# Three PSUM banks shared by all askers, queries by eight heads through DRAM, and a new instruction order in a two-attention kernel

## The chip, the cores and the metric

The kernel runs on one core of one Trainium2 chip. The metric is the device time of one launch in microseconds. The shown time of the kernel before is the median of three runs, 826.01 us (825.94 to 826.19). One execution was profiled; its own time and span are in the table below.

## The reference

Two attentions over the same input `x` (2048 tokens, width 512, 32 heads of 16) are mixed token by token:

```python
g = sigmoid((x * gate_w).sum(-1, keepdims=True))
a = softmax(q k^T / 4) v, per head, over all 2048 keys, then @ A_wo
b = softmax over 8 neighbours (token, token-2, ... token-14) of q k / 4, weighted v, then @ B_wo
out = g * a + (1 - g) * b
```

`q`, `k`, `v` come from `x @ A_wqkv` and `x @ B_wqkv`. `B_x` is not used. All inputs are bf16.

## The kernel before, in words

**Attention A** is cut into 32 periods: 4 blocks of 512 queries, and in each 8 groups of 4 heads. A period needs 64 units; a unit is one head with 128 keys and 512 queries. For a unit TensorE multiplies `kt_all` with `qt` into PSUM (scores, 32 rows per head), an engine takes the exponential, and TensorE multiplies the result with `vp_all` into the accumulator of the period. ScalarE takes most units: sets of three and two in turn stand in two PSUM rings (`rA`, three banks, and `rB`, two), and one ACTIVATE turns a set into a `pT` buffer (three buffers for each ring, so set k writes the buffer of set k-6). VectorE takes 339 units in all (3 to 12 in a period, `n_dve`): it scales the scores of one unit and adds a constant so that, read as bf16 bits, they are a rough exponential (`p1`, out of PSUM bank `D` into `dt_a` or, late, `wkv`), and for three units together it makes three shifted copies (`sh`, into `pd_a`); the four copies are multiplied with four weighted versions of V (`vd_all`), which smooths the error of the rough exponential. At a period's end VectorE transposes the accumulator (`accT`), takes reciprocals (`rden`), GpSimd scales (`ott`), and VectorE transposes back (`oat`).

**Queries.** `q_proj` (L721) makes a period's `qt`: 16 matmuls of 32 columns, in which every head's 16 columns stand twice (`wq2`); VectorE copies the result out of PSUM and masks the sign of the second copy with `qmask` (it carries an upper bound of the scores).

**Attention B** goes in 16 tiles of 128 tokens (`b_tile`). TensorE projects keys, values and queries; VectorE copies them out; keys and values go to a DRAM scratch `kv_scr` and come back shifted by 0 to 14 tokens (`ksh`, `vsh`, four shifts in one load, three buffers `gat`). GpSimd forms the products with the query, adds them up in halves to logits `lg`, subtracts the maximum; ScalarE takes the exponential; GpSimd multiplies with the gate and the reciprocal, forms the products with V and adds them up to `obb`. TensorE transposes `obb`, and the output projection adds it to attention A's part.

**Order.** Every instruction belongs to an `Op` with an engine, a duration, a due time, dependencies and buffers. `list_schedule` (L159) runs once while the kernel is built: it goes forward in planned time, and of the operations of an engine that can start it takes the one due first. It puts in matmuls with zeros where TensorE would idle. The result is a fixed order on each engine; chained helpers (L323, and L332 for matmuls) force it, so nearly all instructions carry these two lines. An engine whose next instruction must wait holds up all behind it. The DMAs of the kernel are all issued by SP, in its own fixed order.

**PSUM.** Eight banks: five for the rings, one `acc` (the accumulator), one `D` (scores for VectorE) and one `misc` (all projections, transposes, outputs, zeros).

Of the kernel before, what the change touches and what calls it, by code (L numbers as in the profile page):

```python
# [20 lines left out]
    dve_tiles=3,  # L21
# [15 lines left out]
DEXP = 56  # L37
NV = 4
NGR = 3
NPD = 3  # L40
# [4 lines left out]
NDE = 2  # L45
NDL = 4
SPREAD = (0.75, 0.8)
STEP = 32.0
WEIGHTS = (0.240234375, 0.2021484375, 0.169921875, 0.142578125)
# [10 lines left out]

class Tok:
    def __init__(self, res):
        self.res, self.ops = res, []


class Op:

    def __init__(self, eng, occ, fn, dl, deps=(), alloc=(), use=(), lat=None, rel=0.0, name="",
                 mode="f", js=(), full=0.0, fill=False, scores=None, after=(), ride=False, parts=None):
        self.scores, self.ride, self.parts = scores, ride, parts  # L70
# [17 lines left out]
GFIRST = -300.0  # L88
PRE = 0.14
GP = lambda kind, n: [(False, PRE), (True, NS[kind] * n)]  # L90
# [11 lines left out]
P1D, SHD, LASTD, PO1D = -100.0, 2.0, 200.0, 300.0  # L102
# [56 lines left out]
def list_schedule(ops, zeros):  # L159
# [15 lines left out]

    def avail(o):
        t = o.ready
        for tk in o.alloc:
            r = tk.res
            n = len(r.order)  # L180
            if n >= r.cap:
                for u in r.order[n - r.cap].ops:
                    if u.done is None:
                        return INF
                    t = max(t, u.end + SELF[u.eng] if u.eng == o.eng else u.done)
        return t

    arr = Array()

    def start(e, o):  # L190
# [5 lines left out]
        t0, end, _, _ = arr.plan(o, t)  # L196
        rides = o.mode == "r" and arr.mode == "r" and end < arr.end + 0.05
        return t0, o.dl + ((ALONE if o.ride else KEEP) if o.mode != arr.mode else 0.0) - (RIDE if rides else 0.0)
# [3 lines left out]
    while len(out) < len(ops):  # L202
# [24 lines left out]
        if e == "pe":  # L227
            tz, n = arr.idle(o, t)
            if n > 0:
                z = zeros(n)  # L230
                tz = max([tz, avail(z)] + [u.t for tk in z.alloc[0].res.order[-2:] for u in tk.ops if u.done is not None and u.t < t])
                if tz + n * PASS + (0.0 if o.mode == "c" else SWITCH) <= t + 0.05:
                    for tk in z.alloc:
                        tk.res.order.append(tk)
# [3 lines left out]
        for tk in o.alloc:  # L238
            tk.res.order.append(tk)
# [16 lines left out]
        out.append(o)  # L256
        for s_ in succ.get(o, ()):
            left[s_] -= 1
            if left[s_] == 0:
                s_.ready = max([s_.rel] + [d.end + SELF[d.eng] if d.eng == s_.eng else d.done for d in s_.deps] + [d.t for d in s_.after])  # L260
# [5 lines left out]
def kernel(  # L266
# [29 lines left out]

    def misc_ps(shape, dtype=FP32, tag="misc"):
        return ps.tile(shape, dtype, tag=tag, bufs=1, name="misc_ps")
# [50 lines left out]
    def op(eng, occ, fn, dl, **kw):  # L349
        if any(tk.res is res.get("misc") for tk in kw.get("use", ())):  # L350
# [7 lines left out]
    def tok(tag, cap):  # L358
        if tag not in res:
            res[tag] = Res(cap)  # L360
        return Tok(res[tag])
# [30 lines left out]
    for pi, (own, groups) in enumerate(seq):  # L392
        n = sum(len(g) for g in groups)
        left = [(gi, u_) for gi, g in enumerate(groups) for u_ in g]
        total, taken = len(own), 0
        for t, j in own:
# [4 lines left out]
            if left and n - len(left) < n * taken / (SPREAD[n // 10] * total) and all(u_[0] == pi for u_ in cur):  # L401
                js = [u_[2] for u_ in cur]
                pick = [x for x in left if x[0] == left[0][0] and x[1][1] not in js]
                if not pick and n - len(left) + 1 < n * taken / (SPREAD[n // 10] * total):
# [12 lines left out]
    wq2 = const.tile([128, DC, H, 2, DH], BF16, name="wq2")  # L417
# [6 lines left out]
    NH = NG // 2  # L424
    woarr = const.tile([128, NH, D], BF16, name="woarr")
    ident = const.tile([128, 128], BF16, name="ident")
    identf = const.tile([128, 128], FP32, name="identf")
    rowc = const.tile([128, 3], FP32, name="rowc")
    wts = const.tile([128, NV], BF16, name="wts")
# [7 lines left out]
    vd_all = const.tile([128, NV, NTD, H, DH + 1], BF16, name="vd_all")  # L437
# [5 lines left out]
    pd_a = const.tile([128, NPD * NGR * ROW], BF16, name="pd_a")  # L443
# [3 lines left out]
    pd_bufs = [pd_a[:, k_ * NGR * ROW:(k_ + 1) * NGR * ROW].rearrange("p (q n) -> p q n", q=NGR) for k_ in range(NPD)]  # L447
    stage = [pd_a[:, k_ * DC * D:(k_ + 1) * DC * D].rearrange("p (c n) -> p c n", c=DC) for k_ in range(2)]
    ott2 = const.tile([128, 2, BPC, 32], BF16, name="ott2")
# [3 lines left out]
    e1 = const.tile([128, NT], FP32, name="e1")  # L453
    d1 = const.tile([128, NT], FP32, name="d1")

    def init_dve():
# [9 lines left out]
        for m in range(NV):  # L466
            V.memset(wts[:, m:m + 1], WEIGHTS[m] * 2.0 ** -DEXP)

# [10 lines left out]
    def init_pool2():  # L479
        make_identity(nc, identf[:])  # L480
# [19 lines left out]
    def load_x(sc):  # L500
        def s():
            xl = work.tile([128, W // 2, D], BF16, name="xld", tag="gat", bufs=NGA) if sc < NGA else stage[1]
# [4 lines left out]
    wst = {}  # L507

    def load_w(part):
        def s():  # L510
            if part == 0:
                wst["q"] = stage[0]
                out = wst["q"]
            else:
                out = wkv[:, :, (part - 1) * D:part * D]
# [18 lines left out]
    tw = tok("pd", NPD)  # L534
# [7 lines left out]
    o_wq = op("sp", 0.5, load_w(0), -8.5, lat=12.5, alloc=[tw])  # L542
# [13 lines left out]
    def q2(E, i):  # L556
        def s():
            a0 = wst["q"][:, :, 4 * i * DH:4 * (i + 1) * DH]
# [6 lines left out]
    o_q2 = [op("dve", 0.5, q2(V, 0), 0.0, deps=[o_wq], use=[tw])]  # L565
    o_q2 += [op("pool", 1.5, q2(G, i), 4.0 + i, deps=[o_wq, o_k3[1]], use=[tw]) for i in range(1, NG)]
# [5 lines left out]
    o_warm = op("pe", 4.0, warm, -9.0, deps=[o_init_d], alloc=[tok("misc", 1)])  # L572
# [34 lines left out]
    def k_proj(i, sc, tag, dl, rel=0.0):  # L607
        st = {}
        tk = tok(tag, 1)
# [16 lines left out]
    def k_bound(i, dl):  # L626
        st = {}
        tk = tok("acc" if i == 0 else "misc", 1)
# [28 lines left out]
    for i in range(NG):  # L657
        o_kc[i] = []
        for sc in range(NC):
            if i == 0:  # L660
                o_kc[i].append(k_proj(i, sc, ("misc", "acc", "D", "misc")[sc], -2.0 + sc))
# [7 lines left out]
    def v_proj(h0, h1, tb, TB, tag, dl, rel=0.0):  # L669
        n = (h1 - h0) * DH  # L670
        st = {}
        tk = tok(tag, 1)
# [18 lines left out]
        def evd():  # L691
# [3 lines left out]
                            in0=_ap(vp_all[:, t0, h0, 0:1], [list(vp_all[:].ap[0]), [0, NV], [H * (DH + 1), nt], [1, n_]]),  # L695
                            in1=_ap(w, [list(w.ap[0]), [1, NV], [0, nt], [0, n_]]), op=ALU.mult)
# [7 lines left out]
        if nt > 0:  # L704
            d = op("dve", 0.0, evd, dl + 2.0, deps=[c], parts=TT(NV * nt * (h1 - h0) * (DH + 1)))
# [15 lines left out]
    def q_proj(pi, tag, dl, rel=0.0):  # L721
        c_, i = periods[pi]
        st = {}
        tk = tok(tag, 1)
        tq = tok("qt", 3)
        q_tok[pi] = tq

        def part(c0, c1):
            def s():
                if c0 == 0:  # L730
                    st["p1"] = misc_ps([128, QW], tag=tag)
                    qt_tiles[pi] = work.tile([128, QW], BF16, name="qt", tag="qt", bufs=3)
# [17 lines left out]
    for pi in range(1, NP):  # L750
        q_proj(pi, "misc", S0[pi] - 10.0, rel=S0[pi - 1] - 6.0 if pi > 1 else Q1REL)
# [3 lines left out]
    tzp, tzr = tok("misc", 1), tok("misc", 1)  # L755
# [10 lines left out]
    def zsig():  # L766
        A.activation(out=e1[:], in_=st_g["zp"][:, 0:NT], func=ACT.Exp, scale=-1.0)

    def zgate():
        V.tensor_scalar_add(out=d1[:], in0=e1[:], scalar1=1.0)  # L770
        V.reciprocal(out=g_sp[:], in_=d1[:])
        V.tensor_tensor(out=omg[:], in0=e1[:], in1=g_sp[:], op=ALU.mult)

    def zrows():
        st_g["zr"] = misc_ps([128, NT, TPC])
        for s_ in range(TPC):
            for j in range(4):
                mm(st_g["zr"][32 * j:32 * j + 32, :, s_], identf[:, 32 * s_:32 * s_ + 32], g_sp[:], True, True,
# [16 lines left out]
    WH = W // 2  # L795
# [3 lines left out]
    def b_tile(t):  # L799
# [26 lines left out]
        tk = tok("misc", 1)  # L826
# [3 lines left out]
        tk = tok("misc", 1)  # L830
        a = op("pe", WAVE(2), proj("pv", 2, 0), tb - 32 - KB, full=2, deps=[o_bw] + o_xt[cb], alloc=[tk], rel=rel)
# [8 lines left out]
        tk = tok("misc", 1)  # L840
# [12 lines left out]
        tlg, tob, tbb = tok("lg", 2), tok("ob", 1), tok("obb", 1)  # L853
# [4 lines left out]
        def logits_mul(hf, wp, w_, c0):  # L858
            def s():
                if hf == 0 and wp == 0 and w_ == 0 and c0 == 0:  # L860
                    st["lg"] = work.tile([128, H, W], FP32, name="lg", tag="lg", bufs=2)
                if w_ == 0 and c0 == 0:
                    st["prod", hf, wp] = work.tile([128, WP, D], FP32, name="prod", tag="prod", bufs=2)
# [29 lines left out]
        def sm_sub():  # L893
            lg, mx = st["lg"], st["mx"]
            mx_bc = _ap(mx[:], [list(mx[:].ap[0]), [1, H], [0, W]])
            G.tensor_tensor(out=lg[:], in0=lg[:], in1=mx_bc, op=ALU.subtract)
# [12 lines left out]
        def sm_gate():  # L909
            rr = st["rr"]  # L910
            G.tensor_scalar(out=rr[:], in0=rr[:], scalar1=omg[:, t:t + 1], scalar2=None, op0=ALU.mult)

        def sm_mul():
            ex, rr = st["lg"], st["rr"]
            rr_bc = _ap(rr[:], [list(rr[:].ap[0]), [1, H], [0, W]])
            G.tensor_tensor(out=ex[:], in0=ex[:], in1=rr_bc, op=ALU.mult)
# [3 lines left out]
        def av_mul(hf, wp, w_, c0):  # L920
            def s():
                if wp == 0 and w_ == 0 and c0 == 0:
                    key = ("ob", "obb")[hf]
                    st[key] = work.tile([128, D], (FP32, BF16)[hf], name=key, tag=key, bufs=1)
                if w_ == 0 and c0 == 0:
                    st["prod", hf, wp] = work.tile([128, WP, D], FP32, name="prod", tag="prod", bufs=2)
# [4 lines left out]
                G.tensor_tensor(out=st["prod", hf, wp][:, w_, c0:c0 + HB].rearrange("p (h d) -> p h d", d=DH),  # L931
                                in0=st["vsh", hf][:, wp + w_, c0:c0 + HB].rearrange("p (h d) -> p h d", d=DH),
                                in1=attn_bc, op=ALU.mult)
            return s, "bf", HB

        def av_add(hf, wp, c0, k_):
            def s():
                prod, ob = st["prod", hf, wp], st["ob"]
                cs = slice(c0, c0 + HB)
                if not hf and not wp:  # L940
                    G.tensor_tensor(out=ob[:, cs], in0=prod[:, 0, cs], in1=prod[:, 1, cs], op=ALU.add)
                elif k_ == 0:
                    G.tensor_tensor(out=prod[:, 0, cs], in0=prod[:, 0, cs], in1=prod[:, 1, cs], op=ALU.add)
                else:
# [425 lines left out]
```

## Time and profile before

| what | value |
|---|---|
| median of three runs | 826.01 us |
| the profiled execution | 826.04 us |
| its span, first to last instruction | 824.3 us |
| granted TensorE clock, mean | 0.994 |
| exponentials of attention A on ScalarE | 684, in 778.8 us busy |
| first of them starts, last of them ends | 19.67 us, 815.5 us |
| products and adds of 128x256 on GpSimd (`prod<-prod`, `prod<-ksh,qb`, `prod<-vsh,lg`) | 352, 256 and 256 times |
| shifts of VectorE (`pd_a`) | 195 and 144 times, 941 and 945 ns |
| transfers | 47.37 MB, 57 GB/s on average |

Busy times are the union of an engine's records. TensorE's matmuls are pipelined, so a busy TensorE need not be at its peak. "Idle before, <- releaser" is the time in which an engine did nothing ahead of an instruction, put down to whatever came last of what it waited for. Idle time matters only on the chain that ends last.

### The profile page before, as it was taken

The numbers are of one execution on the slowest core, as the hardware profiler recorded it, in microseconds if no ns is written. First come the engines' busy times: TensorE is split into PE (matmuls) and PEld (weight loads), VectorE is DVE, ScalarE is ACT, GpSimd is POOL, SyncE is SP. The second block draws the span as 40 slices with busy tenths as digits, with TensorE's granted clock in tenths as the row PEclk, the third lists the DMA queues.
The fourth block names the chain that finished last, engine by engine and source line by source line (L and its number), as shares of the span: only waits on it lengthen the run. The fifth ranks groups of instructions, "written<-read, shape, count | busy, mean of one in ns | idle before, by whom it ended". The sixth has DMA issues, their size and how long they took to land.

```text
span 824.3 us, 18657 instructions
## 1 busy us (share of the span) xinstructions
PE 777.9 (94%) x7314; PEld 247.4 (30%) x7358; DVE 706.3 (86%) x1111; ACT 785.9 (95%) x706; POOL 720.4 (87%) x1196
## 2 busy tenths in 40 slices
PE   7999999999999999999999999999999999999996
PEld 4333433333322222222222222222222222222231
DVE  5456876788978999989999899999989899998987
ACT  3899999999899899999999999999999999999995
POOL 5097999999999999899999999899999999899960
PEclk9899999999999999999999999999999999999999
DMA  9203020112111220211112111211111211110000
GB/s 296 78 3 116 2 90 28 65 52 65 57 48 65 65 66 28 63 53 47 63 35 77 57 50 51 65 53 49 43 52 54 82 34 65 52 52 27 27 1 26
DMA packets 44440, 47.37 MB, mean 57 GB/s; under 512 B 2352, under 2 KB 41776, under 8 KB 44352
## 3 DMA queue, kind: packets, MB, share of 16 engines
q1 hardware_dynamic: 44352, 46.18, 17.6%
q8 instruction: 57, 0.93, 0.5%
q14 instruction: 31, 0.25, 0.1%
HBM read 39.85 MB, written 6.32 MB: 56 GB/s over the span
## 4 chain that ended last, share of the span: by engine, by line
ACT 47%; PE 31%; issue 18%; DVE 2%; DMA 1%; SPq 0%; DVEq 0%; ACTq 0%
ACT pT L323 46%; PE acc L332 11%; PE ring L332 9%; PE misc_ps L332 8%; PE D L332 3%; DMA xld<-in_A_x_dram 1%; ACT lg L323 1%; DVE pd_a L323 0%; DVE kt_all L323 0%; PE pxt L584 0%; PE misc_ps L1011 0%; DVE dt_a L323 0%; DVE qt L323 0%; DVE vp_all L323 0%; DVE wkv L323 0%
## 5 line engine op out<-in xcount | busy, mean ns | idle before, releaser
L323 ACT ACTIVATE pT<-ring 128x1536 bf16<-128x1536 f32 (+1 forms) x684 | 778.8, 1319 | 20.5 <-PE acc L332 14.0
L332 PE MATMUL ring<-qt,kt_all 32*128 32x512 bf16 x1709 | 272.0, 382 | 28.4 <-ACT pT L323 19.2
L323 POOL TENSOR_TENSOR prod<-prod 128x256 f32<-128x256 f32 x352 | 235.6, 677 | 13.2
L332 PE MATMUL acc<-pT,vp_all 128*17 128x512 bf16 (+1 forms) x1709 | 189.0, 385 | 0.3 <-DVE accT L323 0.2
L323 POOL TENSOR_TENSOR prod<-ksh,qb 128x256 f32<-128x256 bf16 x256 | 166.5, 673 | 22.5 <-DMA ksh<-kv_scr 21.7
L323 DVE TENSOR_SCALAR pd_a<-dt_a 128x1536 uint16<-128x1536 uint16 x195 | 180.4, 941 | 1.2
L332 PEld LDWEIGHTS <-kt_all 32*128 32x128 bf16 x2048 | 91.2, 91 | 294.1 <-issue 285.2
L323 DVE TENSOR_SCALAR dt_a<-D 128x512 uint16<-128x512 f32 x195 | 132.7, 680 | 39.2 <-PE D L332 38.5
L323 POOL TENSOR_TENSOR prod<-vsh,lg 128x256 f32<-128x256 bf16 x256 | 162.0, 652 | 0.0
L323 DVE TENSOR_SCALAR pd_a<-wkv 128x1536 uint16<-128x1536 uint16 x144 | 131.0, 945 | 1.9 <-PE acc L332 0.3
L332 PE MATMUL acc<-pd_a,vd_all 128*17 128x512 bf16 x1017 | 130.0, 381 | 0.0
L332 PE MATMUL D<-qt,kt_all 32*128 32x512 bf16 x339 | 128.7, 380 | 1.0 <-DVE kt_all L323 0.4
L323 DVE TENSOR_SCALAR wkv<-D 128x512 uint16<-128x512 f32 x144 | 98.2, 682 | 7.5 <-PE D L332 5.9
L332 PE MATMUL misc_ps<-z 128*32 128x512 bf16 x260 | 85.3, 387 | 1.6 <-DVE z L323 1.6
L332 PEld LDWEIGHTS <-vp_all 128*17 128x17 bf16 (+1 forms) x1709 | 43.7, 88 | 74.9 <-issue 66.6
L332 PEld LDWEIGHTS <-vd_all 128*17 128x17 bf16 x1356 | 42.3, 88 | 64.3 <-issue 51.5
L332 PE MATMUL misc_ps<-bw,xT 128*128 128x512 bf16 x162 | 51.6, 393 | 2.4 <-DVE kt_all L323 0.8
L323 POOL TENSOR_TENSOR ob<-ob,prod 128x256 f32<-128x256 f32 x64 | 45.5, 729 | 0.0
L332 PEld LDWEIGHTS <-z 128*32 128x32 bf16 x341 | 29.9, 96 | 42.2 <-issue 26.1
L332 PEld LDWEIGHTS <-xT 128*128 128x128 bf16 x576 | 30.2, 98 | 36.8 <-issue 31.8
L332 PE MATMUL misc_ps<-xT,wq 128*32 128x512 bf16 x512 | 40.5, 382 | 0.1
L323 DVE TENSOR_SCALAR_CACHE_REDUCE kt_all<-misc_ps,rowc 128x512 bf16<-128x512 f32 x32 | 23.8, 746 | 16.0 <-PE misc_ps L332 15.4
(85 smaller groups left out, 611.9 us busy)
## 6 DMA issues: line engine op xcount, KB each, us to landing
ksh<-kv_scr SPq DMA_DIRECT2D x32, 512.0 KB, 3.9
vsh<-kv_scr SPq DMA_DIRECT2D x32, 512.0 KB, 3.7
kv_scr<-kvs SPq DMA_DIRECT2D x16, 256.0 KB, 2.0
out_dram<-osb SPq DMA_DIRECT2D x16, 128.0 KB, 1.7
xld<-in_A_x_dram SPq DMA_DIRECT2D x3, 512.0 KB, 6.4
bw<-in_B_wqkv_dram SPq DMA_DIRECT2D x1, 1536.0 KB, 11.5
wkv<-in_A_wqkv_dram SPq DMA_DIRECT2D x2, 512.0 KB, 7.3
pd_a<-in_A_x_dram SPq DMA_DIRECT2D x1, 512.0 KB, 8.4
```

The costliest lines, as they stand in the source:

```text
L323: return chain_on(key, f(*a, **k))
L332: return chain(nc.tensor.matmul(out, lhsT=lhsT, rhs=rhs, start=start, stop=stop, **kw))
```

## The change

1. `misc`, `acc` and `D` become one class `Banks`: three banks, and whoever asks gets the one that is free first. At most two may be accumulators, so that a period's accumulation can begin before the last one's is transposed.
2. From the third period on, queries are made for two periods (eight heads) at once: four full matmuls, one copy, one masking without `qmask`; both versions are stored to a DRAM scratch `q_scr` and come back as two `qt` tiles with the heads' rows in the right places. There are four `qt` buffers, not three. Only two of eight weight groups are still doubled in `wq2`.
3. The planner gets margins: what waits for GpSimd is planned 3 to 4 us after GpSimd's planned end, and what GpSimd gets from VectorE 1.5 us later. An accumulation that lies four or more sets behind the newest exponential gets 100 us of extra urgency.
4. GpSimd's sums over the neighbours: the first four products go into one buffer `av`, the others into `prod` (three buffers); then adds of four at a time. A form that would sum by DMA is there, but its condition (`t < -1`) never holds. The counts of products and adds stay.
5. VectorE's rough exponential: a new offset lets the unshifted copy use `vp_all` itself, so `vd_all` holds three weighted versions, for four key tiles in place of three; the number of units stays 339. One early and three late buffers (two and four before); the score matmul itself waits for the buffer. In the last period its units are spread over 60% of the sets (`SPREAD`), in periods with 12 of them over 88% (80% before). `LASTD` goes.
6. Buffers `obt`, `oat`, `accT` and `ott` become single; the output projection is due earlier.

```diff
-DEXP = 56
+DEXP = -2.0565
-NDE = 2
-NDL = 4
-SPREAD = (0.75, 0.8)
+NDE = 1
+NDL = 3
+SPREAD = (0.75, 0.88, 0.6)
...
+class Banks(Res):
+    def __init__(self, n):
+        super().__init__(1)
+        self.banks = [[] for _ in range(n)]
...
+NPR = 3
+MARGIN = {("pool", "pe"): 4.0, ("pool", "dve"): 3.0, ("pool", "act"): 3.0, ("pool", "sp"): 3.0, ("dve", "pool"): 1.5}
+QD = 20.0
+PVU, PVN = 100.0, 4
...
+    def known(d, o):
+        if d.eng == o.eng and not d.far:
+            return d.end + SELF[d.eng]
+        return d.done + MARGIN.get((d.eng, o.eng), 0.0)
...
+            t = max(t, min(freed(o, b, 1) for b in r.banks) if isinstance(r, Banks) else freed(o, r.order, r.cap))
...
+        urge = PVU if o.of is not None and last[0] - o.of >= PVN else 0.0
...
+    def q_pair(pi, dl, rel):
...
+                    mm(st["p"][:], wq[:, c, 4 * i * DH:4 * (i + 2) * DH], xT[:, c, c_ * QW:(c_ + 1) * QW], c == 0, c == DC - 1)
...
+                SP.dma_start(out=_ap(q_scr[8 * pi + e:8 * pi + e + 1, :], [[2 * DH * QW, 8], [QW, DH], [1, QW]]),
+                             in_=src[:])
...
+                SP.dma_start(out=qt_tiles[pi + e][:], in_=_ap(q_scr[8 * (pi + e):8 * (pi + e) + 1, :], [[QW, 128], [1, QW]]))
...
+    for pi in range(2, NP, 2):
+        q_pair(pi, S0[pi] - QD, S0[pi - 2] - 2.0)
...
-            ps_ = mulp(av_mul, hf, wp) + [av_add(hf, wp, c0, k_) for k_ in k1 for c0 in range(0, D, HB)]
...
-            aseq += [gs_[k_] for k_ in (0, 2, 4, 1, 3, 5, 6, 7) if k_ < len(gs_)]
...
+        tav = tok("av", 1)
...
+            if hf:
+                b = sums_of(wp, [b], [tav, tp_])
+                sums.append(b)
+        a1 = sums_of(None, sums, [tav])
...
-        tx = tok("D", 1)
+        tx = tok("misc", 2)
...
-            a = op("dve", 0.0, sh(m, pb), tn + 1.5 + SHD * (m - 1) - (LASTD if late and gi == n_dve[pi] // NGR - 1 else 0.0), deps=deps, alloc=[tp], use=[g["td"]], lat=0.065 + NGR * QW / 1920.0 + SH_LAT, after=d_sh[-1:],
...
+                a = op("dve", 0.0, sh(m, pb), tn + 1.5 + SHD * (m - 1), deps=list(g["p1"]), alloc=[tp], use=[g["td"]],
...
-        dl = E + (4.0 + 4.0 * tt if last else 10.0 + 14.0 * tt)
+        dl = E + (4.0 + 4.0 * tt if last else 2.0 + 4.0 * tt)
```

More of the change, by code (lines that the diff above doesn't have):

```diff
@@ L179, in avail, with take @@
             r = tk.res
[L180 to L185, printed above, removed]
-        return t
-    arr = Array()
+            t = max(t, min(freed(o, b, 1) for b in r.banks) if isinstance(r, Banks) else freed(o, r.order, r.cap))
+        return t
+    def take(o):
+        for tk in o.alloc:
+            r = tk.res
+            if isinstance(r, Banks):
+                tk.bank = min(range(len(r.banks)), key=lambda b: freed(o, r.banks[b], 1))
+                r.banks[tk.bank].append(tk)
+            r.order.append(tk)
+    arr, last = Array(), [0]
     def start(e, o):
@@ L256, in list_schedule @@
         out.append(o)
+        if e == "act" and o.of is not None:
+            last[0] = o.of
         for s_ in succ.get(o, ()):
@@ L937, in s, with av_sum @@
+        def av_sum(wp):
             def s():
[L938 to L945 removed]
```

369 lines of the change are left out of this document (228 added, 141 removed).

## The prediction

> **What bounds the kernel now.** I read the profile from the engine totals to the waits of the fullest engine, and from there to the stretches where it waits. The totals come first:
>
> ```profile
> PE 777.9 (94%) x7314; PEld 247.4 (30%) x7358; DVE 706.3 (86%) x1111; ACT 785.9 (95%) x706; POOL 720.4 (87%) x1196
> ```
>
> ScalarE (ACT) is fullest. Its work is fixed: 342 exponentials of three units, 341 of two and one of one unit, and the diff leaves their number alone. In the steady stretches the ends of two neighbouring ones lie 1.343 us (three units) or 0.917 us (two) apart, so they need 342 x 1.343 + 341 x 0.917 + 0.5 = 772.5 us, and 16 small softmax exponentials add 16 x 0.3 = 4.8. The first starts at 19.67 us and the last ends at 815.5 us. That is 795.8 us for 777.3 us of work; 824.3 - 815.5 = 8.8 us follow as a tail. So what can be won is ScalarE's idle time between 19.67 and 815.5. Its waits say what it is (who waited <- for whom: us in total, times, longest):
>
> ```profile
> ACT pT L323 <- PE acc L332: 14.0, 9, 3.1
> ACT xT L323 <- PE pxt L584: 8.4, 4, 3.9
> ACT pT L323 <- PE ring L332: 5.7, 2, 5.2
> ```
>
> The second row and 5.2 of the third lie before the first exponential. The first row is the matter: nine times an exponential could not write its `pT` buffer because TensorE had not yet read it for the accumulation. With 0.5 and 0.3 from smaller rows ScalarE idles **14.8 us** after its start. One such stretch (busy us by engine, in order of names PE, PEld, DVE, ACT, POOL):
>
> ```profile
> 203.00:211.00 8.00, 7.49 (x92) 3.25 (x90) 7.63 (x14) 4.06 (x5) 7.76 (x13) 1.00 0.25 68
> ```
>
> TensorE is full and ScalarE half idle: it is an order in which TensorE does other work first. GpSimd is nearly full too, and must not be forgotten:
>
> ```profile
> POOL lg L323 <- DVE mx L323: 10.2, 14, 2.3
> ...
> POOL rr L323 <- DVE rr L323: 4.9, 10, 0.9
> POOL rden L323 <- DVE rden L323: 4.9, 11, 0.8
> POOL rr L323 <- ACT pT L323: 2.1, 3, 1.0
> ```
>
> **Part 1: the stalls in TensorE's order (banks, urgency, query pairs).** Every engine's order is fixed when the kernel is built, so it can be read before a run. Exponential k takes the `pT` buffer of k-6. I counted, in the built order, the matmuls that stand between the score matmuls of k and the last accumulation that reads `pT` of k-6. Before, eight or more stand there at exponentials 7, 8, 63, 64, 102, 157, 158, 159, 212, 213, 529, 660 and 661 (56 of them at 158: keys, queries, zeros). The trace idles there and nowhere else by over 0.7 us: 3.1 us at number 7, 1.8 at 63, 2.0 and 2.1 at 157 and 158, 2.2 at 212, 1.2 at 529, 1.3 at 660. So this count is a faithful reading of the order. In the changed order it finds **none**. The extra weight for late accumulations and the pairs (4 full matmuls for two periods in place of 2 x 16 strip matmuls; 16 strips take 1.05 us, so 15 x 0.9 = 13 us of TensorE go) explain why.
>
> What is left is score matmuls that come late. For that I priced all matmuls between successive score matmuls from rows (strip of 16: 0.055 each; full 128x512: 0.22; zero 0.215; score group with its change of mode 0.33) and set the sum over three sets against the exponentials that cover it. Before, the excess was 3.2, 2.0, 1.9, 1.5, 1.3 and 1.2 us at the places above, and about as much was lost; at the places with 0.5 to 0.7 between nothing and 0.4 was lost. After, the largest are 1.9 us (exponential 123, 24 key strips in one run) and 1.1 us (665), five are 0.75 to 0.9 and seven 0.5 to 0.65. I price these as 1.6 + 0.9 + 5 x 0.2 = **3.5 us**. Gain 14.8 - 3.5 = 11.3 us; its bounds are 14.8 (nothing left) and 14.8 - 11.2 = 3.6 (every excess lost in full); I stay near the upper one because places with 0.5 to 0.7 lost little before.
>
> **Part 2: GpSimd's order and margins.** The count of 224 adds and 256 products with V stays; 12 of its 14 copies of query weights (0.34 us apart) go; they end before 18 us, after which GpSimd waits until 39.3 us for the first `ksh`: nothing. Before, its finished blocks (`obb`) lie 46.3 to 47.3 us apart. The changed order puts the transposes that read them nearer: by exponential numbers (1.13 us each) the fourteenth must be ready about 11 us sooner than before, GpSimd must need some 45.8 us per block, and TensorE, which is in order, would wait if not. Where does GpSimd get it? An add right behind the product that it reads starts 0.72 us after it, one behind an unrelated product 0.60; before, 119 adds stand so, after, four products go ahead of four adds: 119 x 0.12 = 14 us, 0.9 per block. The four wait rows above are 22.1 us, 1.4 per block; margins of 1.5 us (VectorE to GpSimd) cover most of the 0.7 us average. 46.9 - 0.9 - (0 to 1.4) is 44.6 to 46.0, so it just fits at the worst end; margins of 3 to 4 us for those who wait for GpSimd come on top of the 1.1 to 4.9 us between block and transposes in the trace. Cost **0**, at the worst 3 us (below, the GpSimd rival).
>
> **Part 3: queries through DRAM.** VectorE loses 30 copies (0.684) and 30 maskings (0.538) and gains 15 of each: -18.3 us of 706.3. That lies beside ScalarE: 0. SP gains 60 transfers of 128 KB. The trace has no such round trip; the nearest rows are a 256 KB store that lands in 2.0 us and a 512 KB load in 3.9. Copy, masking, store and load are at most 0.7 + 0.5 + 2.0 + 3.9 + four issues of 0.4 = 8.7 us. By the order a pair's matmuls stand 16 exponentials (18 us) ahead of the first use in the worst pair, 20 or more in the others. What can eat the 9 us is SP's own queue: loads of `vsh` that wait for GpSimd (421.9 us over 47 waits, longest 12.9) stand ahead of the stores. Worst case 4 us once; below nothing it cannot go, as the tile is only needed then. I take **0**. The first pair also stands ahead of `bwo` and `woarr` in that queue; they are read only after 200 us, and the first `kv_scr` store still waits for a copy at about 32 us, as it does now (32.91).
>
> **Part 4: the end.** The last period's score blocks for VectorE bunch up. After the last of their matmuls (behind score set 680 of 684 in both orders) VectorE has three shifts before, seven after. Shifts run 0.89 us apart (three in 2.67). Before, this is the end:
>
> ```profile
> 811.52 2.67 DVE L323 TENSOR_SCALAR pd_a<-wkv 128x1536 uint16<-128x1536 uint16 x3
> ...
> 816.06 0.72 DVE L323 STREAM_TRANSPOSE accT<-acc 128x512 f32<-128x512 f32 x1 [1.86 <-PE acc L332]
> ```
>
> VectorE idles 1.86 us ahead of the final transpose. Four more shifts cost 3.6; the matmul comes 0.6 sooner; 3.6 - 0.6 - 1.9 = 1.1, and the last shift's matmuls (0.4, and the wait for them 0.4) follow it: **+1.9 us** (0 to 4). At the head, the second V projection no longer waits 0.8 us for its bank: -0.2.
>
> **Sum.** Span 824.3 - 11.3 + 1.9 - 0.2 = 814.7; 826.04 - 824.3 = 1.74 us lie around it (the profiled execution, 826.04, is 0.03 above the median of the runs, 826.01): **816.4 us**.
>
> **Rivals.** *All stalls gone*: 814.7 + 1.7 - 3.5 = 812.9, or 811 without the tail; chance 0.12. *GpSimd gains nothing* and sets the pace at 46.9: block 15 would end at 118.6 + 14 x 46.9 + 20.2 = 795.4; its transposes stand 10 exponentials from the end (11.3), the tail is 10.7: span 817.4, time 819.1; chance 0.08. Against it speak the dependent adds. *The clock.* From 25 to 32 us, behind 64 one-column matmuls, TensorE ran at half clock:
>
> ```profile
> 25.00:32.00 7.00, 6.01 (x34) 1.60 (x32) 1.89 (x5) 3.94 (x5) 0.00 (x0) 0.51 0.00 0
> ```
>
> ScalarE lost 3.1 us in those 7. The change spreads those matmuls over exponentials 18 to 25 with zeros between, so it may lose this stall or move it. If three banks in turn let the clock fall elsewhere, each 7 us at half clock cost some 3: one gives 819.5; chance 0.08. The Trainium skill (TensorE: Matmul & The Clock Gate, "A second HAM failure mode: psum-queue depth-cycling") speaks against the change here: cycling through PSUM banks may leave small idle gaps between groups and make the clock oscillate. The trace doesn't bear it out so far: the granted clock stays 1.00 from 32 us on, over two ring tiles used in turn.
>
> *Slower: GpSimd lags more.* If regrouped products and adds wait more (one `av` buffer in place of two `prod`), the same formula passes 827.7 at 47.5 us per block, 0.6 above today's; at 48.0, as between the second and third block of the trace, it gives 118.6 + 672 + 20.2 + 22.0 + 1.7 = 834.5. Chance 0.09. *It doesn't do what it says*: the stalls return at other places through bank waits on VectorE, 14.8 us as before, and the tail stays: 826.04 + 1.9 = 827.9; chance 0.05.
>
> **Numbers.** Forecast 0.58 (811 to 820). About 0.2% (1.7 us) is what a measurement can tell from no change. Faster: 0.58 + 0.12 + 0.08 + 0.08 = 0.86; slower 0.09 + 0.02; the rest, 0.03, within. The range 810 to 822 holds the forecast and the three milder rivals; it leaves out the two slow cases and the far end of the lost excesses (826.04 - 3.6 + 1.7 = 824.1).
>
> **What would show it.** ScalarE's wait for `PE acc` falls from 14.0 to under 3; blocks of GpSimd 44.6 to 46.0 apart, and no TensorE wait for GpSimd above 0.5 us; no wait of score matmuls for a query load; VectorE without idle time ahead of the last transpose, and more than 10 us from the last exponential to the end. A ScalarE that waits over 8 us in total after its first exponential would prove me wrong.

## The result, and the profile after

The changed kernel takes **817.51 us** (median of four runs, 817.27 to 817.56) against 826.10 us for the kernel before on the same chip: ratio 0.9895, 95% interval 0.9878 to 0.9912. Forecast were 816.4 us, 810 to 822. The profiled execution took 817.27 us with a span of 815.5 us.

I cut the span in three: up to the first exponential, from there to the end of the last one, and the rest.

| us | before | after | change |
|---|---|---|---|
| start to first exponential | 19.67 | 19.30 | -0.37 |
| first exponential to end of last | 795.82 | 786.42 | -9.40 |
| tail | 8.77 | 9.77 | +1.00 |

The engine totals of the changed kernel:

```profile
PE 748.7 (92%) x6963; PEld 244.7 (30%) x7018; DVE 687.5 (84%) x1080; ACT 786.0 (96%) x706; POOL 712.0 (87%) x1184
```

ScalarE is as busy as before (785.9 us), VectorE 18.8 us less. TensorE's busy time is not to be read to the microsecond: of one and the same TensorE order e10 below recorded 7018 matmuls and 756.9 us, as records are missing.

The waits of ScalarE (ACT) and GpSimd (POOL), in the form who waited <- for whom: us in total, times, longest:

```profile
POOL lg L364 <- DVE mx L364: 9.7, 15, 2.0
ACT pT L364 <- PE ring L373: 9.3, 9, 5.1
...
ACT xT L364 <- PE pxt L622: 8.2, 4, 3.7
...
POOL rden L364 <- DVE rden L364: 6.8, 17, 0.9
...
POOL rr L364 <- DVE rr L364: 3.7, 10, 0.7
```

The row for accumulations, 14.0 us before, is gone (0.9 us, once, is left under `misc_ps`). Of `PE ring` 5.1 us lie before the first exponential, so 4.2 us in eight waits stand behind it (before 0.5 in one): score matmuls that come a little late. In all ScalarE idles 5.2 us in nine waits after its first exponential, before 14.8 in eleven. GpSimd's three rows are 20.2 us.

The two stretches shown of before, now (columns in the same order, granted clock and DMA last):

```profile
203.00:211.00 8.00, 7.70 (x64) 2.37 (x62) 7.72 (x14) 7.46 (x9) 7.92 (x12) 1.00 0.29 83
25.00:32.00 7.00, 6.82 (x75) 2.05 (x69) 3.50 (x7) 6.97 (x7) 0.00 (x0) 1.00 0.74 185
```

ScalarE is busy for 7.46 of 8 and 6.97 of 7 us (before 4.06 and 3.94), and the clock stays at 1.00 in the second. The end of VectorE's timeline:

```profile
801.75 5.24 DVE L364 TENSOR_SCALAR pd_a<-wkv 128x1536 uint16<-128x1536 uint16 x6
...
807.47 0.72 DVE L364 STREAM_TRANSPOSE accT<-misc_ps 128x512 f32<-128x512 f32 x1 [0.48 <-PE misc_ps L373]
```

Six shifts follow each other and VectorE idles 0.48 us ahead of the last transpose, in place of three and 1.86 us.

### The profile page after: what moved, and what is told of

The parts are those of the page before. It is cut to its first block, busy times and chain, and to the rows that moved or that the text cites. A ratio compares the mean times of both kernels' runs of the same rounds, so it can differ in the third digit from the quotient of the medians.

```text
span 815.5 us, 18105 instructions
## 1 busy us (share of the span) xinstructions
PE 748.7 (92%) x6963; PEld 244.7 (30%) x7018; DVE 687.5 (84%) x1080; ACT 786.0 (96%) x706; POOL 712.0 (87%) x1184
## 4 chain that ended last, share of the span: by engine, by line
ACT 45%; PE 27%; issue 18%; DVE 6%; POOL 3%; DMA 1%; SPq 0%; DVEq 0%; ACTq 0%
ACT pT L364 45%; PE misc_ps L373 19%; PE ring L373 8%; DVE pd_a L364 2%; POOL av L364 2%; DVE wkv L364 1%; POOL prod L364 1%; DMA xld<-in_A_x_dram 1%; ACT lg L364 1%; DVE dt_a L364 0%; DVE osb L364 0%; PE pxt L622 0%; DVE kvs L364 0%; DVE kt_all L364 0%; DVE oat L364 0%
## 5 line engine op out<-in xcount | busy, mean ns | idle before, releaser
L373 PE MATMUL misc_ps<-pT,vp_all 128*17 128x512 bf16 (+1 forms) x1709 | 208.3, 383 | 0.6 <-DVE accT L364 0.4
L364 POOL TENSOR_TENSOR prod<-prod 128x256 f32<-128x256 f32 (+1 forms) x256 | 163.2, 648 | 6.1
L364 DVE TENSOR_SCALAR wkv<-misc_ps 128x512 uint16<-128x512 f32 x192 | 129.3, 683 | 27.3 <-PE misc_ps L373 23.3
L373 PE MATMUL misc_ps<-z 128*32 128x512 bf16 x421 | 138.5, 386 | 1.6 <-DVE z L364 1.6
L373 PE MATMUL misc_ps<-pd_a,vd_all 128*17 128x512 bf16 x1017 | 131.4, 381 | 0.9 <-DVE pd_a L364 0.5
L373 PE MATMUL misc_ps<-qt,kt_all 32*128 32x512 bf16 x339 | 125.1, 380 | 1.5 <-DVE wkv L364 0.4
L364 DVE TENSOR_SCALAR dt_a<-misc_ps 128x512 uint16<-128x512 f32 x147 | 98.6, 683 | 19.0 <-PE misc_ps L373 17.8
L364 POOL TENSOR_TENSOR av<-av,prod 128x256 f32<-128x256 f32 x128 | 89.6, 727 | 0.0
L364 POOL TENSOR_TENSOR prod<-vsh,lg 128x256 f32<-128x256 bf16 x128 | 79.1, 645 | 0.0
L364 POOL TENSOR_TENSOR av<-vsh,lg 128x256 f32<-128x256 bf16 x128 | 77.6, 642 | 0.0
```

Of the source, the lines that this page charges most:

```text
L364: return chain_on(key, f(*a, **k))
L373: return chain(nc.tensor.matmul(out, lhsT=lhsT, rhs=rhs, start=start, stop=stop, **kw))
```

## The experiments

**Theories.** A: the gain comes out of TensorE's order, and the urgency of late accumulations makes that order. B: relief makes it (less TensorE work by the query pairs, banks that are free). Later M and P, on what the margins do. All orders are rebuilt for each kernel, so a variant that moves one part also shuffles small stalls of 1 to 2 us elsewhere; I read differences below that as the shuffle. The table collects what I read from each profile: the stretch from the first exponential to the end of the last, the tail, the mean distance of GpSimd's blocks from the first to the fifteenth, and VectorE's longest copy within SBUF among key fills (`kt_all<-kt_all`) and query maskings (usually 0.2 to 1.3 us). Each ratio is to the kernel before as measured beside that run (825.69 to 826.17 us).

| kernel | median us | ratio to before (95%) | stretch | tail | block | longest copy |
|---|---|---|---|---|---|---|
| before | 826.10 | 1 | 795.8 | 8.8 | 47.0 | 1.3 |
| changed | 817.51 | 0.9895 (0.9878 to 0.9912) | 786.4 | 9.8 | 46.1 | 1.3 |
| e1 no urgency | 832.22 | 1.0076 (1.0061 to 1.0091) | 803.6 | 8.5 | 46.3 | 1.8 |
| e2 urgency alone | 827.78 | 1.0023 (1.0011 to 1.0036) | 797.5 | 9.1 | 47.0 | 1.2 |
| e3 banks apart | 842.30 | 1.0196 (1.0173 to 1.0220) | 810.8 | 8.5 | 46.1 | 1.6 |
| e4 no margins | 831.91 | 1.0073 (1.0056 to 1.0089) | 811.8 | 8.5 | 48.2 | **9.16** |
| e5 no margins, gaps | **813.15** | 0.9848 (0.9831 to 0.9864) | 783.0 | 8.6 | 46.0 | 1.2 |
| e6 no margins, mask | 820.22 | 0.9929 (0.9915 to 0.9944) | 790.0 | 8.5 | 46.6 | 6.83 |
| e7 strips | 819.78 | 0.9924 (0.9909 to 0.9939) | 789.0 | 9.0 | 46.3 | 2.77 |
| e8 both mendings | 814.13 | 0.9854 (0.9839 to 0.9869) | 783.6 | 8.5 | 46.1 | 1.3 |
| e9 sums interleaved | 818.87 | 0.9917 (0.9901 to 0.9934) | 787.1 | 10.1 | 46.7 | 1.3 |
| e10 margins, gaps | 817.51 | 0.9900 (0.9885 to 0.9915) | 786.4 | 9.8 | 46.1 | 1.3 |

**e1: no urgency.**

```diff
-PVU, PVN = 100.0, 4
+PVU, PVN = 0.0, 4
```

> The changed kernel, only the extra weight of late accumulations set to nothing (PVU 100 to 0); banks, query pairs and margins stay. Theory A (the time comes out of TensorE's order, and the urgency sets that order): in the built order eight or more matmuls again stand between score matmuls and the accumulation they need, at exponentials 7, 8, 16, 17, 201, 202, 370, 371, 533, 538, 539, 660, 661; priced matmul by matmul the excess there is 2.4, 2.4, 3.2, 5.6, 1.3, 3.1 and 2.5 us, 20.5 in all, in place of the 5 to 7 lost now; ScalarE's waits for accumulations come back at those numbers, ScalarE idles 15 to 21 us after its first exponential, and the time is 826 to 833 us. Rival B (the relief does it: 15 pairs take 13 us off TensorE and three banks spare it waits): the stalls stay away, 816 to 820 us. Both leave GpSimd's blocks at 46 us apart or wider.

Measured 832.22 us. The waits are back:

```profile
POOL prod L364 <- DMA ksh<-kv_scr: 25.6, 1, 25.6
...
ACT pT L364 <- PE misc_ps L373: 20.7, 8, 5.7
```

The losses lie where the built order has them: 2.4 us at exponential 7, 2.8 at 16 (the clock is at 0.50 there too, from 37.6 us; the gate's 64 matmuls of one column run from 35.0 to 39.2), 3.3 at 201, 5.8 at 370, 1.2 at 533, 3.0 at 538, 2.6 at 660. The worst stretch, exponential 370, with TensorE full and ScalarE idle:

```profile
450.00:458.00 8.00, 7.59 (x52) 3.13 (x51) 5.46 (x8) 2.29 (x3) 7.84 (x14) 1.00 0.15 50
```

A holds and B falls as far as the pairs and banks alone are meant: without urgency they leave the kernel slower than before.

**e2: urgency alone,** added to the kernel before.

```diff
+        urge = PVU if o.of is not None and last[0] - o.of >= PVN else 0.0
...
-        return t0, o.dl + (...) - (RIDE if rides else 0.0)
+        return t0, o.dl + (...) - (RIDE if rides else 0.0) - urge
```

> The kernel before with the urgency alone: no shared banks, no query pairs, no margins, neighbour sums as before. Theory A (order): its built order has no place with eight or more matmuls, the largest excesses are 1.7 (exponential 163), 1.6 (25), 0.96, 0.8, 0.8 us, priced 3 to 5 us of idle ScalarE in place of 14.8; the tail keeps its three last shifts. If GpSimd has room, the time is 826.0 - 14.8 + 4 = 815 us. Theory A with GpSimd as the next bound: its fifteenth block must now be ready for transposes at 765 us, at 46.9 us per block it ends at 118.6 + 14 x 46.9 = 775; then TensorE waits for GpSimd, in all some 5 to 10 us of ScalarE are lost again, and the time is 819 to 823 us, with waits of TensorE for GpSimd in the trace. Rival B (relief and banks): the stalls stay or move, 823 us or more, without waits for GpSimd.

Measured 827.78 us: A alone falls too. ScalarE idles 14.7 us after its first exponential, as before. No wait of ScalarE for an accumulation is over 0.9 us, but score matmuls come late in another way, 4.07 us at exponential 25 and 3.36 at 163, where the order alone showed 1.6 and 1.7. The timeline of TensorE (PE) and VectorE (DVE) at exponential 25:

```profile
49.66 1.05 PE L337 MATMUL misc_ps<-xT,wq 128*32 128x512 bf16 x16 [0.26 <-DVE kt_all L328]
...
50.75 0.69 DVE L328 CAST qt<-misc_ps 128x512 bf16<-128x512 f32 x1 [0.76 <-PE misc_ps L337]
...
51.50 0.19 PE L337 MATMUL misc_ps<-kmax_b,perm 128*128 128x1 bf16 x2 [0.58 <-DVE qt L328]
52.09 0.21 DVE L328 SCALAR_TENSOR_TENSOR negk<-misc_ps,rowc 128x1 f32<-128x1 f32 x1
52.34 0.96 DVE L328 TENSOR_SCALAR kt_all<-kt_all,rowc,negk 128x2048 bf16<-128x2048 bf16 x1
...
53.85 2.37 ACT L328 ACTIVATE pT<-ring 128x1536 bf16<-128x1536 f32 x2 [3.96 <-PE ring L337]
```

The two small matmuls for the key bound need the one `misc` bank, which holds the next query projection until VectorE has copied it out; behind them wait the bound, the key fill, and the scores of a new group of heads. A count of matmuls sees none of that: a chain through one bank costs latency, not work. GpSimd's blocks lie 47.0 us apart as I feared, but TensorE waited for them only 2.4 us in eight waits. The one-column matmuls still come bunched (48 from 21.8 to 24.5 us), and the clock still falls, at 22.4 us, when the first 16 of them are done (third column from the end):

```profile
22.00:25.00 3.00, 3.00 (x59) 1.65 (x56) 0.90 (x1) 3.00 (x3) 0.00 (x0) 0.56 0.09 27
```

**e3: banks apart.**

```diff
-        name = "banks" if tag in ("misc", "acc") else tag
+        name, cap = tag, (1 if tag in ("misc", "acc", "D") else cap)
...
-        tx = tok("misc", 2)
+        tx = tok("D", 1)
```

> The changed kernel with the three PSUM banks given out as before (one for accumulations, one for VectorE's score blocks, one for the rest); urgency, query pairs, margins stay. Theory A (order, in which the banks are only a constraint): the built order has eight or more matmuls at exponentials 169, 170, 212, 213, 378, 399, 545, 546, 669, 670, excess 4.4 (215), 3.0, 3.0, 2.8, 1.6, 1.6 us, 16 in all; the time is 826 to 831 us although urgency and pairs are there. Theory A weakened (the urgency alone decides): 816 to 820 us. Tail: four last shifts in place of six, so about 1 us shorter than in the changed kernel.

Measured 842.30 us, beyond the forecast of 826 to 831: the counted places cost more than their matmuls (6.8 us at exponential 212, where the largest price was 4.4, at 215), and 25 and 163 lose 3.9 and 5.6 us as in e2. At 212:

```profile
282.03 0.71 DVE L363 STREAM_TRANSPOSE accT<-misc_ps 128x512 f32<-128x512 f32 x1
...
282.79 0.40 PE L372 MATMUL misc_ps<-pT,vp_all 128*32 128x512 bf16 x4 [0.25 <-DVE accT L363]
...
283.28 2.37 ACT L363 ACTIVATE pT<-ring 128x1024 bf16<-128x1024 f32 x2 [6.65 <-PE misc_ps L372]
```

Here a period changes. The first accumulation of the new one needs the one accumulator bank, that waits for its transpose, this for the last shifted scores of the old period, and meanwhile the `pT` buffers fill up. With shared banks two accumulations can overlap. So urgency and banks are both needed: urgency without banks is e2 and e3, banks without urgency e1. That the two suffice is not shown: no run adds both alone to the kernel before, and no run takes points 5 and 6 of the change out of the changed one.

**e4: no margins.**

```diff
-MARGIN = {("pool", "pe"): 4.0, ("pool", "dve"): 3.0, ("pool", "act"): 3.0, ("pool", "sp"): 3.0, ("dve", "pool"): 1.5}
+MARGIN = {}
```

> The changed kernel with all planned margins for and of GpSimd taken out. TensorE's built order is a little better (largest excess 1.45, 0.9, 0.6 us, then none above 0.6, in place of 1.9, 1.1, five of 0.75 to 0.9). If the margins buy nothing (GpSimd keeps its pace and nobody waits for it), ScalarE idles 2 us less and the time is 815 to 816 us. If the margins are what keeps others from waiting for GpSimd, the spare time of 7 to 11 us between a block and its transposes goes, as do the 7 to 8 us ahead of the softmax exponentials, single waits of 0.5 to 3 us for GpSimd show on ScalarE, VectorE or TensorE, and the time is 818 to 823 us.

Measured 831.91 us. The profiled execution took 841.42 us (span 839.5) and the other four 831.43 to 832.72, so the losses read from this trace hold some 10 us more than the median. Neither case had this. TensorE waits for GpSimd 2.2 us in all; the losses are four blows of 2.3 to 8.1 us with what follows on them, and they begin on VectorE:

```profile
113.80 9.16 DVE L364 TENSOR_SCALAR kt_all<-kt_all,rowc,negk 128x2048 bf16<-128x2048 bf16 x1
122.88 0.68 DVE L364 CAST vp_all<-misc_ps 128x512 bf16<-128x512 f32 x1
```

The key fill takes 9.16 us in place of 0.8. Three query maskings take 4.16, 5.06 and 5.89 us in place of 0.5; the longest:

```profile
600.55 5.89 DVE L364 TENSOR_SCALAR qa<-qs 128x256 uint32<-128x256 uint32 x1
```

GpSimd's timeline beside the key fill:

```profile
114.42 2.78 POOL L364 TENSOR_TENSOR av<-av 128x256 f32<-128x256 f32 x4
117.15 1.41 POOL L364 TENSOR_TENSOR obb<-av 128x256 bf16<-128x256 f32 x2
118.51 2.55 POOL L364 TENSOR_TENSOR prod<-ksh,qb 128x256 f32<-128x256 bf16 x4
121.01 2.52 POOL L364 TENSOR_TENSOR prod<-prod 128x256 f32<-128x256 f32 x3
```

All of these follow without a gap (the next starts 0.05 us before the end of the one ahead), up to the third `prod<-prod`, which reads the sum made right ahead of it and starts at 122.49, 0.08 us behind it. The fill ends 0.47 us after that. The three maskings end 0.07 us behind such a start. A second price comes with it: TensorE stands still for 7.3 us behind VectorE, and the granted clock falls to half in the middle of that, at 119.5 us, and stays there until 133.1:

```profile
119.00:126.00 7.00, 2.39 (x20) 0.38 (x19) 7.00 (x5) 0.69 (x1) 6.92 (x9) 0.53 0.00 0
126.00:133.00 7.00, 7.00 (x50) 1.65 (x46) 4.34 (x9) 5.47 (x5) 6.76 (x13) 0.50 0.24 77
```

So a new theory, P: a copy of VectorE within SBUF can be kept out as long as GpSimd's instructions follow each other without a gap. The regrouped sums of the change made these runs long: 6.0 us at most in the kernel before, 20.5 us in the changed one, 26 us here. Rival M: late results of GpSimd are the loss. The next runs test it from both engines.

**e5: no margins, with gaps in GpSimd's order** (e4 plus this; the same sums in another order).

```diff
-            for w_ in range(WP):
-                for c0 in range(0, D, HB):
+            for w_, c0 in ([(1, HB), (1, 0), (0, HB), (0, 0)] if wp is not None else [(0, 0), (0, HB), (1, HB), (1, 0)]):
+                if True:
```

> The run without margins again, all other orders unchanged, except that GpSimd's neighbour sums run in another order within each group of four: the first sum of a group is the one that reads the product made right ahead of it, and the first of the last two additions follows the sum that it reads. The traces show a gap of 0.08 us ahead of such an instruction, and none (the next starts 0.05 us before the end) between independent ones. Theory P (VectorE's copies within SBUF, the key fill of 2048 columns and the query masking, cannot start while GpSimd's instructions follow each other without a gap; in the run without margins they took 9.16, 5.89, 5.06 and 4.16 us in place of 0.5 to 1.0, and TensorE and ScalarE stood behind them, then at half clock): none of them takes over 5 us, the large stalls of ScalarE go, and the time is 811 to 817 us, below the changed kernel, as the order without margins has less excess. Rival M (without margins GpSimd's results come late, and that is the loss): nothing changes, 829 to 840 us.

Measured 813.15 us, faster than both kernels; its interval does not meet that of the change. GpSimd's longest run without a gap is 8.6 us, and the same fill now is

```profile
113.91 1.04 DVE L364 TENSOR_SCALAR kt_all<-kt_all,rowc,negk 128x2048 bf16<-128x2048 bf16 x1
```

The orders of TensorE, VectorE, ScalarE and the transfers are those of e4, so 18.8 us hang on the place of a few sums. P holds, M falls. The totals:

```profile
PE 744.1 (92%) x6948; PEld 245.5 (30%) x7007; DVE 685.4 (85%) x1080; ACT 785.7 (97%) x706; POOL 713.4 (88%) x1184
```

**e6: no margins, masking from PSUM** (e4 plus this; GpSimd's sums in the form of e4).

```diff
-            V.tensor_scalar(out=st["a"][:].bitcast(U32), in0=st["s"][:].bitcast(U32), scalar1=0x7FFF7FFF, scalar2=None,
-                            op0=ALU.bitwise_and)
+            V.scalar_tensor_tensor(out=st["a"][:], in0=st["p"][:], scalar=rowc[:, 0:1], in1=st["s"][:], op0=ALU.mult, op1=ALU.max)
...
-        b = op("dve", 0.0, ab, dl - 6.8, deps=[c], alloc=[tqa], use=[tqs], parts=SB(QW))
+        b = op("dve", 0.61, ab, dl - 6.8, deps=[c], alloc=[tqa], use=[tqs, tk])
```

> The run without margins, GpSimd's order unchanged, but the query masking reads PSUM beside the copy in SBUF (the larger of minus the projection and its copy, the same result) in place of a copy within SBUF. Theory P: the masking takes 0.7 us everywhere, and the three stalls behind it (2.3, 4.8 and 4.8 us, with the half clock after each) go: 815 to 824 us; the key fills stay open to the same wait, and one of them may still take several us. Rival M (late results of GpSimd): 829 us or more, with the stalls where they were. If it is VectorE's load as such that made those copies long, the masking stays long too.

Measured 820.22 us. The edit also tells the planner a new duration and holds the PSUM bank until the masking is done, so all orders are rebuilt; GpSimd's differs from that of e4 in 193 of 1184 places, although the expectation takes it for unchanged. So the time against e4 is not the masking's form alone. What the trace shows of the form: the masking takes 0.71 to 0.75 us in all 15 cases, although 10 of them begin inside runs of GpSimd of 5.7 to 17.7 us without a gap, and the three blows behind it are gone. One of them, with 14 us of such a run still to come, and a key fill, left as it was, that is caught again:

```profile
348.90 0.74 DVE L364 SCALAR_TENSOR_TENSOR qa<-misc_ps,rowc,qs 128x512 bf16<-128x512 f32 x1
...
116.78 6.83 DVE L364 TENSOR_SCALAR kt_all<-kt_all,rowc,negk 128x2048 bf16<-128x2048 bf16 x1
```

The fill ends as in e4, 0.5 us behind the start of the next dependent sum of GpSimd, and ScalarE loses 6.1 and 1.6 us behind it. So the form of the copy decides on VectorE's side, and the gaps on GpSimd's.

**e7: strips in place of pairs.**

```diff
-POOL_G, NPG = (), 1
+POOL_G, NPG = (), 0
...
-    wq2 = const.tile([128, DC, 8, 2, DH], BF16, name="wq2")
+    wq2 = const.tile([128, DC, H, 2, DH], BF16, name="wq2")
...
+    o_q2 += [op("pool", 1.5, q2(G, i), 4.0 + i, deps=[o_wq, o_k3[1]]) for i in range(2, NG)]
...
-    for pi in range(2, NP, 2):
-        q_pair(pi, S0[pi] - QD, S0[pi - 2] - 2.0)
+    for pi in range(2, NP):
+        q_proj(pi, "misc", S0[pi] - 10.0, rel=S0[pi - 1] - 10.0)
```

> The changed kernel with the queries of each period made by 16 strips and masked in place, as before, not by pairs through DRAM (asked for 10 us before the period ahead begins); banks, urgency, margins, neighbour sums as in the change. TensorE gets back 15 x 0.9 = 13 us of work, VectorE 15 copies and 15 maskings (18 us), GpSimd its 12 query copies ahead of its first block, SP loses 60 transfers. Theory A (order): the built order has one place with over eight matmuls (exponential 115) and excesses of 2.5, 1.9, 1.3, 1.1, 0.9, 0.9, 0.8 us; 1 to 3 us more idle time than in the changed kernel: 818 to 821 us. Rival B (the relief of TensorE pays the gain): 826 us or more.

Measured 819.78 us, as A has it. VectorE is at 706.9 us again (before 706.3), and the time is 2.3 us above the changed kernel, hardly more than the shuffle: as far as this run tells, the pairs pay about that much of the 8.6 us or less. Part of the 2.3 us is e7's own: one key fill took 2.77 us, and half clock from 320.8 to 324.2 us ends in a wait of ScalarE of 1.3.

**e8: no margins, both mendings** (e5 and e6 together).

> The run without margins with both mendings: GpSimd's sums in the order with gaps, and the masking from PSUM. Theory P: no copy of VectorE over 5 us, largest excess in the order 0.9 us; ScalarE idles 2 to 3 us after its first exponential, GpSimd's blocks 45.5 to 46.3 us apart, the tail 8.5 us: 811 to 815 us, faster than both kernels. If GpSimd's four more gaps per block (0.12 us each, 0.5 per block) make it late, waits of TensorE for GpSimd of 3 to 8 us in all show, and the time is 815 to 820 us. Rival M: 829 us or more.

Measured 814.13 us, no copy over 1.3 us; not faster than e5 (the intervals overlap). With gaps, the other form of the masking has nothing left to win. e8 is also a second test of the gaps: its orders of TensorE, VectorE, ScalarE and the transfers are those of e6, and only GpSimd's sums stand differently. That brings 6.1 us (820.22 to 814.13) and a longest copy of 1.3 in place of 6.83.

**e9: sums interleaved.** In the second half of a block each product is followed at once by the sum that reads it, as before.

```diff
+                if hf:
+                    b = op("pool", 0.0, av_add(wp, w_, c0), tb + 40, deps=[b], use=[tav, tp_], ...)
             if hf:
-                b = sums_of(wp, [b], [tav, tp_])
                 sums.append(b)
```

> The changed kernel with the neighbour sums as before in one respect: in the second half of a block each product with V is followed at once by the sum that reads it (8 dependent pairs per block), not four products and then four sums. Urgency, banks, pairs, margins stay; the largest excesses in TensorE's order are 1.5, 1.3, 1.2, 1.2, 0.9 us (in the changed kernel 1.9, 1.1, 0.9, 0.85, 0.8). The second step of the prediction priced such a pair at 0.12 us, 0.9 us per block: the blocks then lie 46.5 to 47.0 us apart in place of 46.1, the last one ends 6 to 12 us later (788 to 794 us), its transposes stand five exponentials later in the order, and the time is 818 to 823 us, with single waits of TensorE for GpSimd. If the dependent pairs only fill time in which GpSimd waits for VectorE anyway, the blocks stay 46.1 us apart and the time is 817 to 818.5 us.

Measured 818.87 us. Blocks lie 46.7 us apart, 0.6 more than in the changed kernel for eight dependent pairs: 0.08 us each, not 0.12. The last block ends at 792.1 us (781.4), its transposes stand later in the order and the tail grows to 10.1 us. The time is 1.4 us longer, within the shuffle (ScalarE idles 6.0 us after its first exponential in place of 5.2, partly at other places), so no gain in time from the regrouping is shown.

**e10: the changed kernel with the gaps of e5.**

> The changed kernel, margins and all, with nothing but the new order within GpSimd's sums (as in the run with gaps and without margins); the orders of TensorE and VectorE are the changed kernel's, instruction by instruction. If the changed kernel lost nothing to long copies of VectorE (its longest is 1.29 us), this gives 817 to 818.5 us, and the 4 us between it and the run without margins are the price of the margins in TensorE's order (excess 1.9, 1.1 and so on). If it hid losses to them, 813 to 816 us. Longest run of GpSimd's instructions without a gap: 20.5 us in the changed kernel, under 9 us here.

Measured 817.51 us, with the changed kernel's stalls one by one. So the changed kernel lost nothing to long copies, by the luck of where its copies fall, and the 4.4 us between e10 and e5 are the price of the margins in this kernel's orders (in the profiled spans 4.5: 3.4 of stretch and 1.2 of tail). Beside that the margins came with fewer copies in GpSimd's long runs: 6 begin in a run of over 5 us in the changed kernel, 14 in e4. I take that for an accident of the order; no run tests it.

## Why the prediction was right, and where it was off

**Step 1, stalls in TensorE's order.** The mechanism holds: ScalarE's wait for accumulations fell from 14.0 to 0.9 us. The leftover was mis-sized: 5.2 us of idle time in place of 3.5. Of its two large terms, 1.6 us at exponential 123 and 0.9 at 665, both came (1.61 and 1.03), but the small ones took 0.2 to 1.0 us at eleven places in place of 5 x 0.2: 55 lost 0.97 us where the order showed 0.58. The stretch fell by 9.4 us, not 11.3. The reason given, urgency and pairs, was half wrong: the gain needs urgency and banks (e1, e2, e3); the pairs bring some 2.3 us or less (e7). The 3.1 us of the clock rival, lost at 25 to 32 us, are no loss of their own: they are the wait at exponential 7, one of the 14.0 us. How much of them the half clock cost is not shown; e1 loses 2.4 us at exponential 7 at 28 us, with the clock still at 1.00. The half clock itself comes and goes with the order: e1, e2 and e3 have it again, at 38 to 45, 22 to 33 and 44 to 51 us. The Trainium skill's rule in that rival (TensorE: Matmul & The Clock Gate, "A second HAM failure mode: psum-queue depth-cycling") did not come true in the changed kernel, with three banks in turn: its granted clock is 1.00 in every stretch from 17 to 806 us. e7 and e8, with three banks too, fall to half clock once each, for 3.4 us.

**Step 2, GpSimd.** I wrote 44.6 to 46.0 us per block; it was 46.1, and TensorE waited 0.4 us for it, once, so the cost of 0 stands. The pace before, 46.9 in my sums, was 47.0 (118.6 to 776.3 us over 14 blocks), which makes that range 44.7 to 46.1 and the GpSimd rival 1 us later. A dependent pair costs 0.08 us (e9), not 0.12. Blocks end 6.9 to 11.6 us ahead of their transposes (before 1.1 to 4.9): the margins give GpSimd's slack, and take 4.4 us from the time (e10, e5), a term that the sum lacks. What I missed altogether is what regrouping does to VectorE: not a loss here, but 18.8 us in e4 against e5. My slower rival named the right part, the regrouped sums, but had GpSimd itself lag, where it is VectorE that is held up. That the changed kernel was spared is luck, not something that I foresaw.

**Step 3, queries through DRAM.** VectorE lost 18.8 us (forecast 18.3), and no row of the waits has score matmuls waiting for a query load. Right.

**Step 4, the end.** +1.0 us in place of +1.9: six shifts bunch behind the last score block, not seven, and VectorE idles 0.48 us ahead of the last transpose. The head gave 0.37 us, not 0.2. So two signs that I had named failed: VectorE still idles ahead of the last transpose, and the tail is 9.77 us, not over 10.

Against the profiled execution the forecast was 0.9 us low: 1.9 too much gain in step 1, less 0.9 too much cost in step 4 and 0.2 too little at the head. That these errors partly cancel is luck.

## What to carry to other kernels

Count in the built order what stands between a producer and the instruction it frees, but follow each chain through a single bank too: it costs latency that no count of matmuls shows. Where GpSimd and VectorE share a kernel, look at how long GpSimd runs without a dependent instruction, and at each VectorE copy within SBUF that falls there. Before margins are taken out or put in, find out what they hide; here they cost 4.4 us, and without them a wait of 9 us came up.

## What the runs showed of the hardware

**VectorE's copies and GpSimd's runs.** In the before, the changed and the ten test kernels, six key fills and maskings took over 2 us (9.16, 6.83, 5.89, 5.06, 4.16, 2.77). All were in kernels with regrouped sums and without the extra gaps. Each ended 0.15 us (maskings) or 0.55 us (fills) behind the end of a run of GpSimd without a gap; after five of these runs a dependent instruction followed 0.08 us later, after the last one GpSimd fell idle. Two maskings of 1.78 (e1) and 1.60 us (e3) end in the same way, 0.15 us behind a run. The Trainium skill (SBUF — State Buffer, "Who interferes with whom") has the lock: a VectorE copy in a two-port mode and a GpSimd instruction exclude each other for the whole instruction. The traces agree for most copies, which take 0.2 to 1.3 us and so wait for one boundary at most. That a loser can miss twelve boundaries in a row, the page does not say; e4 shows it. VectorE's evictions from PSUM (128x512, 0.63 to 0.69 us) and its shifts (0.89 to 0.96 us in all twelve kernels) were never held up. Why most copies get in at the next boundary (in e7 22 of 43 began inside a run of over 5 us, and one was held) and a few do not, stays open.

**The clock.** Up to the last exponential the granted clock falls to half for 3.4 us or for about two, three or four times that. Where two or more of the four groups of 16 one-column matmuls start 0.8 to 1.4 us apart, half clock comes with them: in the kernel before at 25.1 us, when all 64 are nearly done; in e1 and e3 at 37.6 and 44.4, after 32; in e2 at 22.4, after 16. In the changed kernel and in e4 to e10 they start 2.7 to 3.6 us apart, and it stays at 1.00 there. That the bunch is the cause is not shown: TensorE was shown busy for 3.1 to 3.5 of the last 4 us ahead of these four falls, and e2, e7 and e8 have a half clock of 3.4 us (from 138.4, 320.8 and 669.5 us) with no such matmul near, within 2 us of an idle time of TensorE of 0.8 to 1.0 us. A standstill of TensorE brings it too: 7.3 us in e4 and 5.3 us in e6, and in both the clock falls before the standstill is over.
